# Transposing float32 q and k of the first head pair on TensorE without casts, in an attention and ELU feed-forward kernel

## The chip, the cores and the metric

The kernel runs on one core of a Trainium2 chip. A core has TensorE (PE; matmuls, and transposes as matmuls against an identity, results into PSUM), VectorE (DVE), ScalarE (ACT), GpSimd (POOL), SyncE (SP), and 16 DMA engines that all queues share. The metric is the device time of one execution in microseconds. Before the change it is 305.96 us, the median of three runs (305.51 to 306.67).

## The reference

The inputs are float32: q, k and v of shape (8, 8, 576, 64), that is batch, heads, sequence and head dimension, and two weights, w_in (512, 2048) and w_out (2048, 512).

```
scores = scale * q @ k^T                      # per batch and head
local heads 0-3:   0 <= i - j < 32
strided heads 4-7: i >= j and i % 32 == j % 32
attn = softmax(where(mask, scores, -1e9)) ;  a = attn @ v
x = a.transpose(0, 2, 1, 3).reshape(4608, 512)
h = x @ w_in ;  g = where(h > 0, h, exp(min(h, 0)) - 1)
out = g @ w_out                               # (4608, 512) float32
```

## The kernel before, in words

The program is written out by hand. The text `ORDER` is a list of tokens; the loop at its end calls one small function for each token, and each engine executes its instructions in the order in which the tokens issue them. Nothing is scheduled after that: an engine waits where an input or a buffer isn't ready, and everything behind on the same engine waits with it.

A key such as `0s1` names a pair of heads: batch 0, strided (`s`) or local (`l`), pair 1 of two. For the first two batches q and k are transposed on TensorE (`T`, function `transposes`) and copied out of PSUM to `qT` and `kT` as bfloat16 by VectorE (`c`) or ScalarE (`C`). `S` makes scores (L453), `e` the exponential on ScalarE (L460), `m` the mask on VectorE, `O` the products with ones and v, `n` and `r` a logarithm and an exponential that give the reciprocal of the sums (L551, L556), and `x` multiplies it in and writes `xT` in bfloat16 (L581). Layer 1 (`a` with rows 2 and 3 of `xT`, then `b` with rows 0 and 1, or both in `L`; L608) and layer 2 (`Z`, L642) go over 9 chunks of 512 tokens. The later attention pairs are mixed in between them. `D` tokens issue loads on POOL's queue, which also turn float32 into bfloat16 on the way.

The very first pair, `0s0`, does not wait for POOL's queue. Its q and k are loaded as float32 in two halves each, q by SP's queue and k by ACT's, into `stage`, memory of the later `g[0]` (L293 to L297). Four casts (`K` and `k`, function `cast`, L388) turn the halves into bfloat16 in `qs` and `ks`: q's first half and both halves of k on ScalarE, q's second on VectorE. The second half of k is cast ahead of the first. A half is transposed by four matmuls of 72 columns with the data as the weights (L401) and copied by L421. The other strided pair, `0s1`, is loaded as bfloat16 by POOL's queue ahead of everything else there.

`w` tokens (function `warm`, L385) are matmuls of zeros into a bank that is free. They compute nothing. A number is its columns, so `w.0.512.200` is two of them into bank 0. Eight of 512 columns open the program, and more stand between the steps up to the first `a`.

PSUM has 8 banks of 2 KiB for each partition, and the last number of a `T`, `S` or `O` token names the bank or banks. Four bfloat16 transposes of a half fill 288 columns of 2 bytes.

Of the kernel before, what the change touches and what calls it, by code (L numbers as in the profile page):

```python
# [8 lines left out]
F32 = mybir.dt.float32  # L9
BF16 = mybir.dt.bfloat16  # L10
I32 = mybir.dt.int32
ALU = mybir.AluOpType
# [23 lines left out]
w.7.512.512.512.512.512.512.512.512 D.ql.0.1 F.vp D.kl.0.1 F.v1 D.ql.0.0 k.q.0 F.ms D.vs.0.0 T.0s0.q.0.7  # L36
D.kl.0.0 K.q.1 K.k.1 D.vs.0.1 K.k.0 C.0s0.q.0 w.0.512.512.512.512.512 T.0s0.k.0.6 D.vl.0 T.0s0.k.1.5
T.0s0.q.1.4 c.0s0.k.0 T.0s1.k.7 c.0s0.k.1 c.0s1.k w.0.324 T.0s1.q.6 c.0s0.q.1 D.wi1.0 S.0s0.0.01 c.0s1.q
S.0s0.1.23 e.0s0.0 w.5.185 S.0s1.0.45 D.qs.1 S.0s1.1.67 e.0s1.0 m.0s0.0 w.2.224.224 T.0l1.k.1 D.wi3.0
e.0s1.1 m.0s1.0 w.0.499 T.0l0.q.0 C.0l1.k D.wi0.0 m.0s1.1 T.0l1.q.7 e.0s0.1 c.0l1.q w.4.155 O.0s0.0.16  # L40
D.wi2.0 c.0l0.q n.0s0.0 w.4.314 S.0l1.1.45 S.0l1.0.23 m.0s0.1 F.mk r.0s0.0 T.0l0.k.7 O.0s0.1.60 e.0l1.1
x.0s0.0 D.wo0.0 F.ml e.0l1.0 w.0.224.224.102 O.0s1.1.15 c.0l0.k n.0s0.1 D.wo1.0 w.4.247 O.0s1.0.43
n.0s1.1 m.0l1.0 n.0s1.0 r.0s1.1 D.ql.1 w.2.512.512.108 S.0l0.0.23 x.0s1.1 e.0l0.0 V.0 w.7.512.331
S.0l0.1.01 r.0s1.0 m.0l1.1 r.0s0.1 w.7.512 O.0l1.0.75 m.0l0.0 e.0l0.1 O.0l1.1.32 x.0s1.0 n.0l1.0 m.0l0.1
w.2.224.224 O.0l0.0.10 n.0l1.1 x.0s0.1 r.0l1.0 w.1.142 O.0l0.1.54 r.0l1.1 x.0l1.0 D.ks.1 n.0l0.0
w.4.224.224 a.0.5.6 x.0l1.1 n.0l0.1 a.0.7.7 r.0l0.0 a.0.4.0 r.0l0.1 x.0l0.0 a.0.6.4 D.kl.1 x.0l0.1
T.1s1.q.3 b.0.5 c.1s1.q b.0.7 h.0.5 b.0.4 h.0.7 i.0.5 b.0.6 h.0.4 g.0.5 T.1s0.q.5 D.wo2.0 a.0.12.3
C.1s0.q i.0.4 a.0.13.6 h.0.6 g.0.4 a.0.14.5 b.0.12 a.0.15.2 h.0.12 b.0.15 j.0.6 D.vs.1 a.0.2.1 j.0.12
b.0.13 g.0.6 b.0.2 h.0.13 g.0.12 a.0.1.4 h.0.2 i.0.7 b.0.1 i.0.13 a.0.3.3 g.0.7 h.0.1 D.wo3.0 b.0.3
i.0.2 b.0.14 h.0.3 g.0.2 a.0.0.7 j.0.1 b.0.0 a.0.11.1 g.0.1 h.0.0 a.0.10.0 h.0.14 D.vl.1 i.0.0 b.0.10  # L50
j.0.3 g.0.0 b.0.11 h.0.10 a.0.8.4 g.0.3 b.0.8 h.0.11 g.0.13 Z.0.0.0.7 h.0.15 i.0.10 D.ks.2 i.0.14
Z.0.0.1.7 h.0.8 g.0.10 j.0.11 Z.0.3.0.6 j.0.15 g.0.11 D.vs.2 Z.0.3.1.6 g.0.15 g.0.14 a.0.9.3 D.qs.2
i.0.8 b.0.9 g.0.8 Z.0.1.0.5 h.0.9 j.0.9 T.1s0.k.4 D.kl.2 Z.0.1.1.5 C.1s0.k g.0.9 T.1s1.k.2 S.1s0.1.01
c.1s1.k T.1l1.k.4 e.1s0.1 T.1l1.q.3 c.1l1.k T.1l0.q.2 S.1s1.0.01 m.1s0.1 Z.0.3.2.6 e.1s1.0 C.1l1.q
m.1s1.0 Z.0.1.2.5 C.1l0.q O.1s1.0.43 T.1l0.k.2 n.1s1.0 S.1s1.1.01 c.1l0.k Z.0.0.2.7 e.1s1.1 r.1s1.0
S.1s0.0.01 S.1l1.1.23 x.1s1.0 e.1s0.0 Z.0.1.3.5 m.1s1.1 m.1s0.0 e.1l1.1 Z.0.0.3.7 q.0.1 m.1l1.1 D.kl.3
S.1l0.1.01 S.1l1.0.23 V.1 e.1l0.1 Z.0.3.3.6 q.0.0 e.1l1.0 O.1l1.1.54 X.ks.2 m.1l1.0 O.1s0.1.73 n.1l1.1
m.1l0.1 S.1l0.0.01 n.1s0.1 Z.0.2.0.2 q.0.3 r.1l1.1 r.1s0.1 x.1l1.1 e.1l0.0 O.1s0.0.64 x.1s0.1 O.1l1.0.53
W.2 n.1s0.0 O.1l0.1.71 n.1l1.0 Z.0.2.1.2 m.1l0.0 r.1s0.0 X.qs.2 n.1l0.1 x.1s0.0 r.1l1.0 D.ql.2
O.1s1.1.04 r.1l0.1 x.1l1.0 O.1l0.0.63 n.1s1.1 x.1l0.1 Z.0.2.2.2 n.1l0.0 r.1s1.1 r.1l0.0 Z.0.2.3.2  # L60
x.1s1.1 X.kl.2 x.1l0.0 L.1.12.7 t.0.1 L.1.6.6 h.1.12 i.1.12 L.1.3.5 h.1.6 D.ks.3 i.1.6 L.1.4.4 h.1.3
D.vl.2 g.1.6 L.1.1.3 g.1.12 h.1.4 i.1.3 L.1.5.6 h.1.1 g.1.3 D.vs.3 L.1.13.7 i.1.4 h.1.5 i.1.1 i.1.5
L.1.0.5 h.1.13 g.1.5 D.qs.3 o.0.2 L.1.7.1 g.1.1 j.1.13 D.ql.3 g.1.4 h.1.0 L.1.2.6 X.ql.2 h.1.7 g.1.13
L.1.10.0 j.1.0 i.1.7 h.1.2 g.1.7 L.1.14.7 t.0.2 h.1.10 g.1.0 j.1.2 S.2s1.0.12 S.2s1.1.34 i.1.10 t.0.0
L.1.8.5 g.1.2 e.2s1.1 e.2s1.0 g.1.10 L.1.15.6 t.0.3 h.1.8 m.2s1.1 m.2s1.0 h.1.14 S.2s0.0.01 S.2s0.1.23
X.ks.3 L.1.9.4 e.2s0.1 i.1.14 g.1.14 h.1.15 L.1.11.3 e.2s0.0 i.1.15 h.1.9 Z.1.3.0.7 g.1.15 h.1.11 i.1.8
Z.1.3.1.7 j.1.9 g.1.8 m.2s0.1 O.2s1.1.01 Z.1.2.0.2 i.1.11 n.2s1.1 g.1.9 O.2s0.1.56 r.2s1.1 g.1.11
Z.1.2.1.2 n.2s0.1 x.2s1.1 Z.1.3.2.7 r.2s0.1 m.2s0.0 O.2s1.0.01 x.2s0.1 Z.1.2.2.2 n.2s1.0 O.2s0.0.34
r.2s1.0 Z.1.3.3.7 n.2s0.0 x.2s1.0 Z.1.2.3.2 r.2s0.0 q.1.3 S.2l0.0.01 S.2l0.1.56 x.2s0.0 Z.1.1.0.7
e.2l0.0 q.1.2 e.2l0.1 m.2l0.0 S.2l1.0.01 S.2l1.1.34 X.qs.3 Z.1.1.1.7 m.2l0.1 e.2l1.0 e.2l1.1 m.2l1.0  # L70
O.2l0.0.56 O.2l0.1.01 X.kl.3 n.2l0.0 m.2l1.1 Z.1.0.0.4 n.2l0.1 Z.1.0.1.4 r.2l0.0 t.1.3 O.2l1.1.23
r.2l0.1 x.2l0.0 Z.1.0.2.4 n.2l1.1 x.2l0.1 O.2l1.0.56 r.2l1.1 Z.1.0.3.4 X.ql.3 n.2l1.0 x.2l1.1 Z.1.1.2.7
r.2l1.0 D.qs.4 Z.1.1.3.7 x.2l1.0 D.kl.4 q.1.0 L.2.11.6 W.3 S.3s0.0.01 S.3s0.1.23 h.2.11 L.2.3.5 e.3s0.1
i.2.11 g.2.11 L.2.7.4 D.ks.4 h.2.3 o.1.1 D.vl.3 i.2.3 L.2.2.6 m.3s0.1 e.3s0.0 g.2.3 L.2.5.7 h.2.7 h.2.2
i.2.7 L.2.4.5 h.2.5 g.2.7 j.2.2 i.2.5 L.2.9.3 m.3s0.0 h.2.4 D.vs.4 g.2.5 L.2.0.4 h.2.9 g.2.2 j.2.4
D.ql.4 L.2.14.7 i.2.9 h.2.0 g.2.4 O.3s0.1.01 h.2.14 g.2.9 L.2.10.6 n.3s0.1 i.2.0 L.2.6.5 i.2.14 h.2.10
g.2.0 r.3s0.1 L.2.8.3 i.2.10 X.ks.4 g.2.14 h.2.6 L.2.13.4 x.3s0.1 h.2.8 j.2.6 g.2.10 O.3s0.0.01 X.qs.4
L.2.1.7 n.3s0.0 i.2.8 g.2.6 L.2.15.6 r.3s0.0 g.2.8 t.1.0 h.2.1 L.2.12.5 x.3s0.0 h.2.15 X.kl.4 i.2.1
S.3s1.0.01 S.3s1.1.23 g.2.1 e.3s1.1 Z.2.1.0.7 e.3s1.0 m.3s1.1 i.2.15 h.2.13 m.3s1.0 S.3l0.0.01
S.3l0.1.23 h.2.12 g.2.15 Z.2.1.1.7 e.3l0.1 i.2.12 j.2.13 Z.2.1.2.7 g.2.12 e.3l0.0 g.2.13 O.3s1.1.23  # L80
S.3l1.0.01 S.3l1.1.56 m.3l0.1 n.3s1.1 Z.2.1.3.7 m.3l0.0 e.3l1.1 Z.2.0.0.4 e.3l1.0 m.3l1.1 r.3s1.1
m.3l1.0 O.3s1.0.01 q.2.1 O.3l1.1.56 Z.2.0.1.4 n.3l1.1 x.3s1.1 t.2.1 n.3s1.0 Z.2.3.0.7 r.3l1.1 X.ql.4
O.3l1.0.23 Z.2.0.2.4 r.3s1.0 x.3l1.1 n.3l1.0 x.3s1.0 Z.2.3.1.7 t.1.2 r.3l1.0 S.4s1.0.01 S.4s1.1.56
x.3l1.0 t.1.1 Z.2.0.3.4 e.4s1.1 e.4s1.0 m.4s1.1 O.3l0.1.23 O.3l0.0.56 q.2.0 n.3l0.1 Z.2.3.2.7 W.4
r.3l0.1 Z.2.2.0.4 m.4s1.0 D.vs.5 n.3l0.0 x.3l0.1 O.4s1.1.01 D.ks.5 r.3l0.0 Z.2.2.1.4 D.vl.4 n.4s1.1
x.3l0.0 Z.2.3.3.7 r.4s1.1 L.3.14.6 x.4s1.1 D.qs.5 L.3.2.5 h.3.14 q.2.3 D.vl.5 i.3.14 S.4l0.0.01
S.4l0.1.23 h.3.2 L.3.7.7 g.3.14 e.4l0.0 i.3.2 e.4l0.1 L.3.11.6 D.kl.5 g.3.2 h.3.7 m.4l0.0 S.4s0.0.01
S.4s0.1.23 h.3.11 m.4l0.1 L.3.1.5 e.4s0.1 X.ks.5 e.4s0.0 Z.2.2.2.4 m.4s0.1 i.3.7 j.3.11 m.4s0.0
O.4s0.1.01 Z.2.2.3.4 g.3.11 n.4s0.1 g.3.7 O.4s0.0.23 r.4s0.1 L.3.0.6 n.4s0.0 x.4s0.1 D.ql.5 L.3.5.7
r.4s0.0 q.2.2 h.3.1 L.3.4.1 x.4s0.0 h.3.5 X.qs.5 L.3.6.4 j.3.1 i.3.5 h.3.0 g.3.5 L.3.15.0 h.3.6 g.3.1  # L90
t.2.0 h.3.4 L.3.12.7 i.3.0 h.3.15 g.3.0 t.2.2 L.3.3.5 j.3.4 i.3.6 h.3.12 g.3.4 L.3.8.6 h.3.3 g.3.6 j.3.3
O.4l0.1.12 i.3.12 L.3.10.3 n.4l0.1 g.3.3 L.3.9.4 i.3.15 h.3.8 g.3.15 h.3.10 L.3.13.5 g.3.12 r.4l0.1
h.3.9 Z.3.0.0.0 x.4l0.1 j.3.9 i.3.10 Z.3.2.0.7 D.qs.6 h.3.13 g.3.10 j.3.8 D.ks.6 Z.3.0.1.0 g.3.9 g.3.8
O.4l0.0.12 Z.3.2.1.7 i.3.13 n.4l0.0 X.kl.5 g.3.13 Z.3.0.2.0 r.4l0.0 x.4l0.0 S.5s0.0.34 S.5s0.1.56
Z.3.0.3.0 e.5s0.1 m.5s0.1 S.4l1.0.12 S.4l1.1.56 o.3.0 Z.3.2.2.7 e.4l1.1 e.4l1.0 Z.3.1.0.0 m.4l1.1 X.ql.5
# [638 lines left out]
```

## Time and profile before

| what | value |
|---|---|
| median of the runs, and their spread | 305.96 us, 305.51 to 306.67 |
| the profiled execution | 306.22 us, its span 304.5 us |
| TensorE busy | 297.1 us, 98% of the span |
| VectorE, ScalarE busy | 226.2 us (74%), 228.5 us (75%) |
| first dense layer-1 matmul starts | 18.62 us |
| zero matmuls | 35, from 1.3 to 18.5 us |

The span runs from the core's first to its last instruction; the execution's time is 1.72 us longer. In the lines of a timeline, the first number is the start in microseconds from the beginning of the span, the second the time that the instructions took, then come engine, line of the kernel, operation, and output and input with shape and type; "x2" is a group of two. A bracket gives the idle time of the engine ahead of it and what ended it. In the chain that ended last, a row is start, length, and the engine and line, or the transfer, that the chain passes through. A matmul's time includes its way through the array, so that those in a row overlap.

### The profile page before, as it was taken

How to read it: one execution, taken by the hardware profiler on the slowest of the kernel's cores; microseconds unless marked ns; L12 is line 12 of the kernel's file. 1: busy time of each engine (PE TensorE's matmuls, PEld its weight loads, DVE VectorE, ACT ScalarE, POOL GpSimd, SP SyncE). 2: the span in 40 equal slices, each digit the busy share in tenths (PEclk: the TensorE clock that was granted, in tenths of full speed). 3: DMA queues.
4: the chain of work that ended last, by engine and by line, in shares of the span. 5: the costliest groups of instructions: out<-in, count | busy, mean ns of one | idle time of the engine just before them, and what ended most of it. 6: DMA issues, size and time to landing. Idle time of an engine off the chain costs nothing.

```text
span 304.5 us, 6258 instructions
## 1 busy us (share of the span) xinstructions
PE 297.1 (98%) x2339; PEld 146.8 (48%) x2339; DVE 226.2 (74%) x435; ACT 228.5 (75%) x412; POOL 80.2 (26%) x110
## 2 busy tenths in 40 slices
PE   6999999999999999999999999999999999999994
PEld 2654455445544454445544554445444544444444
DVE  6777968798779978896788878976788358895020
ACT  4778678598879888997989889978777559982101
POOL 8922436830471008530188250000000000000000
PEclk9999999999999999999999999999999999999999
DMA  8999999999899759999899499801120022000053
GB/s 165 190 206 207 207 193 169 169 198 204 158 158 168 128 123 134 162 192 171 196 154 154 61 132 149 195 16 56 38 69 0 2 69 69 2 1 0 4 155 119
DMA packets 107358, 37.63 MB, mean 124 GB/s; under 512 B 89152, under 2 KB 102848, under 8 KB 107328
## 3 DMA queue, kind: packets, MB, share of 16 engines
q0 software_dynamic: 69728, 19.47, 62.3%
q1 hardware_dynamic: 36920, 17.08, 28.4%
q10 hardware_dynamic: 680, 0.69, 0.8%
q8 instruction: 18, 0.29, 0.4%
q14 instruction: 12, 0.10, 0.1%
HBM read 39.53 MB, written 9.44 MB: 161 GB/s over the span
## 4 chain that ended last, share of the span: by engine, by line
PE 86%; DVE 6%; ACT 3%; issue 2%; DMA 2%; ACTq 0%; DVEq 0%
PE ps L642 40%; PE ps L608 33%; PE ps L453 4%; DVE g L636 3%; DVE he L625 2%; PE ps L523 2%; PE ps L516 2%; DMA g<-in_k_dram 2%; PE ps L385 1%; PE ps L672 1%; ACT he L616 1%; PE ps L411 1%; PE ps L496 1%; PE ps L480 1%; ACT ln L551 0%
## 5 line engine op out<-in xcount | busy, mean ns | idle before, releaser
L642 PE MATMUL ps<-w_out_sb,g 128*128 128x512 bf16 x560 | 132.8, 379 | 0.5 <-DVE g L636 0.5
L608 PE MATMUL ps<-xT,w_in_sb 128*128 128x512 bf16 x576 | 130.5, 379 | 0.2 <-DVE g L634 0.2
L616 ACT ACTIVATE he<-ps 128x512 f32<-128x512 f32 x144 | 80.9, 596 | 22.2 <-PE ps L608 20.0
L608 PEld LDWEIGHTS <-w_in_sb 128*128 128x128 bf16 x576 | 55.0, 98 | 64.3 <-issue 1.1
L642 PEld LDWEIGHTS <-g 128*128 128x128 bf16 x560 | 51.1, 98 | 55.7 <-issue 0.8
L636 DVE TENSOR_TENSOR g<-he,ps 128x512 bf16<-128x512 bf16 x92 | 62.0, 684 | 1.9
L581 DVE TENSOR_TENSOR xT<-ps,ln 64x576 bf16<-64x576 f32 (+1 forms) x64 | 42.6, 678 | 20.3 <-ACT ln L556 19.4
L460 ACT ACTIVATE e<-ps 72x576 bf16<-72x576 f32 (+1 forms) x64 | 39.1, 647 | 12.7 <-PE ps L453 11.9
L625 DVE TENSOR_SCALAR he<-he 128x512 bf16<-128x512 f32 x92 | 40.2, 446 | 7.5 <-ACT he L616 6.8
L551 ACT ACTIVATE ln<-ps 64x576 f32<-64x576 f32 (+1 forms) x64 | 36.3, 583 | 10.0 <-PE ps L523 5.0
L634 DVE SCALAR_TENSOR_TENSOR g<-he,ps 128x512 bf16<-128x512 bf16 x52 | 34.8, 682 | 7.2 <-ACT he L623 6.9
L556 ACT ACTIVATE ln<-ln 64x576 f32<-64x576 f32 (+1 forms) x64 | 38.5, 619 | 1.2
L623 ACT ACTIVATE he<-he 128x512 bf16<-128x512 f32 x52 | 32.5, 630 | 1.3 <-DVE g L636 0.8
L648 DVE COPY osb<-ps 128x512 f32<-128x512 f32 x22 | 15.1, 685 | 16.3 <-PE ps L642 16.0
L243 POOL DMA_DIRECT2D ql<-in_q_dram x24 | 20.1, 840 | 7.7 <-DMA vl<-in_v_dram 4.1
L648 ACT COPY osb<-ps 128x512 f32<-128x512 f32 x13 | 7.6, 586 | 17.9 <-PE ps L642 14.1
L250 POOL DMA_DIRECT2D kl<-in_k_dram x24 | 17.8, 747 | 11.4 <-DMA w_out_sb<-in_moe_w_out_dram 3.7
L473 DVE TENSOR_TENSOR pm<-e,mask_l 128x576 bf16<-128x576 bf16 x32 | 14.1, 453 | 6.9 <-ACT e L460 5.3
L467 DVE TENSOR_TENSOR pm<-e,mask_s 72x576 bf16<-72x576 bf16 x32 | 14.2, 451 | 4.3 <-ACT e L460 4.1
L260 POOL DMA_DIRECT2D vl<-in_v_dram x8 | 9.8, 1220 | 9.5 <-PE ps L523 7.2
L233 POOL DMA_DIRECT2D vs<-in_v_dram x8 | 5.2, 652 | 25.6 <-DVE vsp L588 24.7
L516 PEld LDWEIGHTS <-vsp 72*128 72x128 bf16 x192 | 9.1, 98 | 5.5 <-issue 0.4
(93 smaller groups left out, 153.2 us busy)
## 6 DMA issues: line engine op xcount, KB each, us to landing
out_dram<-osb SPq DMA_DIRECT2D x30, 144.0 KB
vl<-in_v_dram POOLq DMA_DIRECT2D x8, 288.0 KB, 8.9
w_in_sb<-in_moe_w_in_dram POOLq DMA_DIRECT2D x4, 512.0 KB, 13.1
w_out_sb<-in_moe_w_out_dram POOLq DMA_DIRECT2D x4, 512.0 KB, 16.8
kl<-in_k_dram POOLq DMA_DIRECT2D x24, 72.0 KB, 7.3
ql<-in_q_dram POOLq DMA_DIRECT2D x24, 72.0 KB, 8.4
ks<-in_k_dram POOLq DMA_DIRECT2D x5, 320.0 KB, 8.2
vs<-in_v_dram POOLq DMA_DIRECT2D x5, 320.0 KB, 9.1
```

Of the source, the lines that this page charges most:

```text
L460: nc.scalar.activation(e[0:R], tiles.pop(("S", key, u))[0:R], ACT.Exp, scale=scale)
L551: nc.scalar.activation(t, s_ps, ACT.Ln)
L556: nc.scalar.activation(t, t, ACT.Exp, scale=-1.0)
L581: nc.vector.tensor_mul(dst, o_ps, rc)
L608: nc.tensor.matmul(tiles["h", ch, m], lhsT=w_in_sb[:, c, m * 128:(m + 1) * 128], rhs=xT[:, c, ch * CHUNK:(ch + 1) * CHUNK], start=(c == 2) ...
L616: nc.scalar.activation(e, tiles["h", i[0], i[1]], ACT.Exp)
L623: nc.scalar.activation(e1, e, ACT.Relu, bias=1.0, scale=-1.0)
L625: eng.tensor_scalar(e1, e, scalar1=1.0, scalar2=1.0, op0=ALU.min, op1=ALU.subtract)
L634: nc.vector.scalar_tensor_tensor(dst, e1, -1.0, h, op0=ALU.mult, op1=ALU.max)
L636: nc.vector.tensor_tensor(dst, e1, h, op=ALU.max)
L642: nc.tensor.matmul(ops, lhsT=g[ch % 2][:, m, kk * 128:(kk + 1) * 128], rhs=w_out_sb[:, m, :], start=(m == 0), stop=(m == MC - 1), skip_gro ...
L648: eng(o_sb, tiles.pop(("o", int(ch), int(kk))))
```

## The change

q and k of pair `0s0` are no longer cast. `transposes` takes the float32 halves straight from `stage`, with a float32 identity of 72 x 72 (a memset on VectorE and a select on POOL, issued at the start), and writes float32 into PSUM: 288 columns of 4 bytes, a bank for each half. The copies out of PSUM stay and now also turn float32 into bfloat16. There are still four transposes to a half. In `ORDER`:

- the four cast tokens go;
- `T.0s0.k.0` moves up behind `T.0s0.q.0`, ahead of the second halves, and its copy `c.0s0.k.0` with it;
- banks of the opening's transposes change (for example `T.0s0.k.1` from 5 to 7, `T.0s1.k` from 7 to 5);
- the zero matmuls are set anew: 1196 columns between the two halves (2560 before), 712 ahead of `T.0s1.k` (0), 774 ahead of `T.0s1.q` (324), 351 between the scores of `0s0` and `0s1` (185), and from there to the first `a` 5001 columns in place of 5738. Two of 224 columns behind `O.0l0.1` go altogether, and others lose some columns or their last piece.

The scores of pair `0s0` use 72 columns of `kT` as weights instead of 128, so that a block doesn't reach into the next half. A few tokens further back move by a place in the text, which leaves the order on every engine as it was. `load` gets a case for halves of w_in that no token uses.

```diff
 ORDER = """
-w.7.512.512.512.512.512.512.512.512 D.ql.0.1 F.vp D.kl.0.1 F.v1 D.ql.0.0 k.q.0 F.ms D.vs.0.0 T.0s0.q.0.7
-D.kl.0.0 K.q.1 K.k.1 D.vs.0.1 K.k.0 C.0s0.q.0 w.0.512.512.512.512.512 T.0s0.k.0.6 D.vl.0 T.0s0.k.1.5
-T.0s0.q.1.4 c.0s0.k.0 T.0s1.k.7 c.0s0.k.1 c.0s1.k w.0.324 T.0s1.q.6 c.0s0.q.1 D.wi1.0 S.0s0.0.01 c.0s1.q
-S.0s0.1.23 e.0s0.0 w.5.185 S.0s1.0.45 D.qs.1 S.0s1.1.67 e.0s1.0 m.0s0.0 w.2.224.224 T.0l1.k.1 D.wi3.0
+w.7.512.512.512.512.512.512.512.512 D.ql.0.1 F.vp D.kl.0.1 F.v1 D.ql.0.0 F.ms D.vs.0.0 T.0s0.q.0.7
+D.kl.0.0 T.0s0.k.0.6 C.0s0.q.0 D.vs.0.1 c.0s0.k.0 w.0.512.512.172 T.0s0.k.1.7 T.0s0.q.1.6 c.0s0.k.1
+D.vl.0 w.0.512.200 T.0s1.k.5 c.0s1.k c.0s0.q.1 w.0.512.262 T.0s1.q.7 D.wi1.0 S.0s0.0.01 c.0s1.q
+S.0s0.1.23 e.0s0.0 w.4.351 S.0s1.0.45 D.qs.1 S.0s1.1.67 e.0s1.0 m.0s0.0 w.2.224.224 T.0l1.k.1 D.wi3.0
...
+    identity_f = consts.tile([RS, RS], F32, tag="identity_f", name="identity_f")
...
+    nc.vector.memset(identity_f, 1.0)
...
+    nc.gpsimd.affine_select(
+        identity_f, identity_f, compare_op=ALU.is_equal, fill=0.0,
+        base=0, pattern=[[1, RS]], channel_multiplier=-1)
...
-    def cast(eng, nm, i):
-        n, f = "qk".index(nm), 2 * NS * D
-        eng(half(raw[nm + "s"][0:RS, 0:f], int(i)), half(stage[0:RS, n * f:(n + 1) * f], int(i)))
-
     def transposes(key, nm, *a):
         P, bank, part = Pair(key), int(a[-1]), a[:-1]
-        t = ps[:, bank, :].bitcast(BF16)[:, 0:S // (1 + len(part))]
+        t = ps[:, bank, 0:W] if part else ps[:, bank, :].bitcast(BF16)[:, 0:S]
...
         if part:
+            n = "qk".index(nm) * 2 * NS * D
+            src = stage[0:RS, n:n + 2 * NS * D].rearrange("p (h f) -> p h f", h=2)
             for i in range(NS // 2):
...
-                nc.tensor.transpose(t[:, i * RS:(i + 1) * RS], src[:, P.head(x), c0:c0 + 2 * D],
-                                    identity[0:RS, 0:RS])
+                nc.tensor.transpose(t[:, i * RS:(i + 1) * RS], src[:, x, c0:c0 + 2 * D], identity_f)
...
-                nc.tensor.matmul(dst, lhsT=P.kT[pr, k0:k0 + 128], rhs=rhs, start=True, stop=True,
+                n = RS if key == "0s0" else 128
+                nc.tensor.matmul(dst[0:n], lhsT=P.kT[pr, k0:k0 + n], rhs=rhs, start=True, stop=True,
                                  skip_group_check=True)
```

## The prediction, made before the changed kernel was run

> **What bounds the kernel now.** I read the page's busy shares first, then the chain that ended last, first whole and then cut to the first 34 us, then the timelines of each engine up to layer 1, and last POOL's waits, which tell when loads landed.
>
> ```profile
> span 304.5 us, 6258 instructions
> PE 297.1 (98%) x2339; PEld 146.8 (48%) x2339; DVE 226.2 (74%) x435; ACT 228.5 (75%) x412; POOL 80.2 (26%) x110
> PE 86%; DVE 6%; ACT 3%; issue 2%; DMA 2%; ACTq 0%; DVEq 0%
> ...
> 1.29 4.75 DMA g<-in_k_dram
> 6.07 1.15 ACT ks L390 x2
> 7.26 0.32 PE ps L401 x4
> 7.60 0.52 DVE kTs L421 x2
> 8.19 0.36 DVE kTs L427
> ...
> 8.57 0.31 DVE qTs L421
> 8.92 0.31 PE ps L453 x8
> ```
>
> TensorE is 98% busy and carries 86% of the chain: what the opening loses, the end loses. The opening is another thing. Up to 8.92 us the chain is a transfer of k (lands at 6.04), two casts on ScalarE, four transposes, and four copies on VectorE; TensorE only fills in. From 8.92 us on the chain is TensorE without a break, but zero matmuls (L385) stand in it, and those only pass time.
>
> ```profile
> 5.61 0.42 DVE L390 CAST qs<-g 72x512 bf16<-72x512 f32 x1
> 8.78 0.45 DVE L425 COPY qTs<-ps 128x576 bf16<-128x576 bf16 x1
> 9.69 1.18 ACT L460 ACTIVATE e<-ps 72x576 bf16<-72x576 f32 x2 [0.28 <-PE ps L453]
> 15.36 0.65 ACT L460 ACTIVATE e<-ps 128x576 bf16<-128x576 f32 x1 [0.21 <-PE ps L453]
> 19.27 0.76 ACT L556 ACTIVATE ln<-ln 128x288 f32<-128x288 f32 x2
> 19.74 0.95 DVE L581 TENSOR_TENSOR xT<-ps,ln 128x288 bf16<-128x288 f32 x2 [0.50 <-ACT ln L556]
> 17.86 0.64 POOL L233 DMA_DIRECT2D xT<-in_k_dram  x1 [2.95 <-DMA w_in_sb<-in_moe_w_in_dram]
> 22.39 0.75 POOL L278 DMA_DIRECT2D w_out_sb<-in_moe_w_out_dram  x1 [2.29 <-DMA w_in_sb<-in_moe_w_in_dram]
> ```
>
> Behind those zeros the real bound from 9.69 to 20 us is ScalarE: in 12.13 to 18.53 us it is busy for 6.03 of 6.40 us (VectorE 5.57), and its next exponential follows the last at once but for waits of 0.28 and 0.21 us. Its last reciprocal (19.27 + 0.76) frees the last xT product, which ends at 19.74 + 0.95 = 20.69; the second half of the first layer-1 tile (`b.0.5`) needs it and starts at 20.77, though the transposes before it were issued by 20.61. So the start of dense layer 1 is set by ScalarE and VectorE, by 0.1 to 0.2 us. POOL's waits date the weights: wi1 by 17.86 us (first use 18.53), wi3 by 22.39 (first use 22.90).
>
> **The change part by part.** *Casts.* Three on ScalarE (0.62 and 1.15 us) and one on VectorE (0.42) go. On the path is the 1.15 us, 6.07 to 7.21. The other 0.62 and the 0.42 lie beside the wait for k and pay nothing.
>
> *Sixteen float32 transposes* take the place of sixteen bfloat16 ones. Each is still one matmul with one weight load of 128 columns. The trace has no float32 matmul, so the price p is bounded: below by the bfloat16 ones, issued every 33 ns (a group of four in 0.13 us); above by four passes of a weight load that nothing overlaps, 4 x 98 ns (mean of the LDWEIGHTS rows) = 0.39 us. I take 0.10 us, the row that it is nearest to: one pass, with a weight load that is not sped up. The Trainium skill, page "TensorE: Matmul & The Clock Gate", section on weight-path perf modes, says that the fast weight load is not used for FP32, and its LDWEIGHTS section gives columns / 1.2, from which an estimate of 107 ns follows; no trace here shows it yet, and by it the sum below would stay within 0.05 us.
>
> *New timeline up to the scores.* The eight opening zeros end at 4.76 (1.26 + 3.50, unchanged). q's first half is there at 4.28. k's first half was issued first on its queue and the trace's landing record has it at 4.62. So `T.0s0.q.0` and `T.0s0.k.0` run 4.76 to 5.56 (8 x 0.10). Zeros of 512 + 512 + 172 columns at 0.42 ns (512 columns every 0.215 us) take 0.50: 6.06. k's second half lands at 6.04, so `T.0s0.k.1` and `T.0s0.q.1` run 6.09 to 6.89. Zeros of 712 columns: 0.30, 7.19. Now `T.0s1.k` meets another load: ks of heads 6 and 7 is issued at 2.13 and takes 5.1 us, 7.2. It starts at 7.25; before, it started at 7.62. This is the new wait, and all of TensorE stands behind it.
>
> From its first weight load to its copy took 0.57 us before (7.62 to 8.19): the copy starts at 7.82 and the next (`c.0s0.q.1`) 0.38 later, 8.20. That one now reads float32 from PSUM. Bounds: 0.22 us until the next copy starts, as before (8.57 to 8.79), or 288/512 of the 0.685 us of the float32 output copies, 0.39; I take 0.33. So `c.0s1.q` starts at 8.53 and ends at 8.98 instead of 9.23. `T.0s1.q`, behind zeros of 774 columns, has ended by 8.3 and doesn't bind. Gain at `S.0s1.0`, hence at ScalarE's exponential at 9.69: 0.25 us, with the quick copy 0.36. I carry 0.3.
>
> *Narrower scores of the first pair* (72 weight columns, not 128): 16 weight loads. The 64-column loads of L411 are issued every 24 ns, the 128-column ones every 33, so nothing to 0.1 us of gain on TensorE, which waits there for VectorE: 0. The dependence on the second half, which the 128 columns had, goes too; but `S.0s0.0` still stands behind `T.0s1.q` in TensorE's order.
>
> *Fewer zeros behind the scores.* 166 columns more before `S.0s1`, 737 fewer from there to `a.0.5`: 0.31 us of TensorE. Bounds 0 and 0.31. I take 0, because ScalarE is back to back and its work isn't less; only the wait of 0.21 us at 15.36, for scores behind zeros that shrink by 108 columns (0.05 us), can give a little.
>
> *A new identity.* VectorE sets 72x72 float32 (some 0.1 us, next to the 0.17 of the 128x128), POOL fills it (0.20 to 0.31, from the iota and the first identity), in front of six attention loads, vl, and the weights. Of POOL's queue, qs and ks are issued ahead of it. The rest start 0.2 to 0.3 later, but they land 5.0 us after issue, then 9 to 16: they queue behind each other, and from 3.0 us the DMA share is at 1 or above. Cost 0; uncovered it would be 0.25 us at wi1, whose slack is 0.67. Every other DMA and every other instruction keeps its place on its queue, SP's included.
>
> *Loads that an earlier TensorE could meet.* kl lands at 3.87 + 5.0 to 5.6 (used at 10.00), vs at 5.08 + 5.6 (11.52), wi1 at 17.86 (18.53), wi3 at 22.39 (22.90). The least slack is about 0.5 us: 0.3 passes, and no more than 0.5 can.
>
> Sum: ScalarE's chain, `b.0.5` and all that follows start 0.3 us sooner; later stages are the same instructions in the same order. The profiled run took 306.22 (span 304.5 plus 1.72), 0.26 over the median of 305.96: 305.9 for that run, 305.65 against the median.
>
> **The rivals.** *Float32 transposes too dear (slower).* Place: between 6.09 and `T.0s1.k`. All 16 stand in TensorE's order ahead of it, so it starts at 4.76 + 0.80 + 16p if that is later than 7.25. Up to p = 0.105 nothing changes, at about 0.125 the gain is gone, and every further 10 ns cost 0.16. At the upper bound of 0.39: 305.96 + 16 x 0.265 = 310.2. For it: four bytes for two. Against: one weight load and one matmul each. The Trainium skill speaks both ways: "FP8 and Floating Point Precision", in its TensorE notes, gives true FP32 four passes, while the terms of "TensorE: Matmul & The Clock Gate" call the transpose mode four times faster for FP32; the first would put p near the upper bound, the second near what I take. No run here shows either yet.
>
> *The zeros count in full.* Then 0.3 + 0.31, cut by wi3 to 0.5: 305.45. Against it the ScalarE rows above.
>
> *No gain arrives* because ks lands 0.3 later or the copies of float32 are slower: 305.96.
>
> *The clock falls back.* The opening zeros took 0.43 us each, later ones 0.215: TensorE starts at half speed. Between 4.76 and 8.4 zeros fall from 2884 to 2682 columns. Should the gate not see enough work, 3.5 us at half speed cost up to 1.7 us: 307.4. Page "TensorE: Matmul & The Clock Gate", Part 4, says that transposes don't count as busy; by zeros alone 1.21 us against 1.13 hardly differ, so it has little chance.
>
> **How the numbers follow.** Forecast 305.65: 0.63. Zeros in full 0.09. No gain 0.10. Dear transposes 0.13, half of them beyond 1.5 us. Clock 0.05. What a measurement of this kernel tells from no change is about 0.5%, 1.5 us. No named case is that much faster; 0.04 for what I don't see. Slower by that: half of the dear transposes and some of the clock, 0.09. Same: 0.87. Range: the runs of before spread over 305.5 to 306.7; 305.0 takes in the zeros in full with half that spread, 306.7 the cheaper half of the dear transposes.
>
> **What would show it.** No casts at L390; eight float32 transposes over some 0.8 us from 6.1; `T.0s1.k` at 7.2 to 7.3, released by the load of ks; the exponential of L460 now at 9.69 at about 9.4; `b.0.5` at about 20.45, still behind xT of VectorE; the same stages after that, 0.3 earlier. Wrong if the transposes are issued further apart than 0.12 us, if zeros run at 0.43 us after 5 us, or if a w_in wait shows on TensorE before 23 us.

## The result, and the profile after

The changed kernel takes 306.59 us in the median of 20 runs (305.99 to 308.29), the kernel before 305.93 in 20 runs beside it. The ratio, worked out from all these runs and not from the two medians, is 1.0028, with a 95% interval of 1.0018 to 1.0038. That is some 0.85 us slower, where 0.3 us faster was forecast. The time lies within the range that I gave, but by luck: its upper end, 306.7, stands for dear transposes, which did not come. The sign is wrong.

The two profiled executions hide this: 306.22 us before and 306.21 after, with the same span. The one of before is 0.29 us above the median of its runs, the one of after 0.38 below. What follows is therefore read from the places where the traces differ, and every verdict on time from many runs.

From the page of the changed kernel: span, busy engines, the busiest DMA queue (packets, MB, and the time that its packets took as a share of 16 engines' span), and the chain by engine.

```profile
span 304.5 us, 6251 instructions
PE 297.1 (98%) x2336; PEld 147.1 (48%) x2336; DVE 225.5 (74%) x435; ACT 226.8 (74%) x409; POOL 81.0 (27%) x111
q0 software_dynamic: 69728, 19.47, 72.0%
PE 82%; DMA 13%; DVE 2%; POOL 1%; issue 1%; ACTq 0%; DVEq 0%
```

The busy shares are as before. Two lines are not. Transfers carry 13% of the chain, against 2% before; but in the second profile of the changed kernel (`after_again` below, an execution of 306.89 us) they carry 2% again, so this share belongs to one execution. And queue q0, which holds POOL's loads, took 72.0% with 69728 packets and 19.47 MB; before it was the same packets and bytes in 62.3%. This one repeats: 71.4% and 63.1% in the second profiles. Nothing more is moved, but moving it takes longer.

The same chain of the changed kernel, cut to the first 48 us (start, length, what):

```profile
1.28 4.70 DMA g<-in_k_dram
6.12 0.46 PE ps L405 x4
6.67 0.47 DVE kTs L424
7.23 1.19 POOL vl L261
...
11.28 16.39 DMA w_in_sb<-in_moe_w_in_dram
...
27.95 17.07 DMA w_out_sb<-in_moe_w_out_dram
...
45.07 1.89 PE ps L646 x8
```

The casts are gone from the opening, as they should be. From 7.23 us on the chain is no longer TensorE but POOL's queue of loads: the issue of vl, then w_in, then w_out, whose last block lands at 45.03 and lets TensorE go on at 45.07.

TensorE, ScalarE, VectorE and POOL of the changed kernel, from their timelines (start, length, engine, line, operation; in brackets the idle time ahead of it and what ended it):

```profile
6.12 0.70 PE L405 MATMUL ps<-identity_f,g 72*128 72x72 f32 x8 [0.49 <-DMA g<-in_k_dram]
6.65 0.47 PE L391 MATMUL ps<-zero 128*128 128x512 bf16 x2
7.29 0.43 PE L411 MATMUL ps<-identity,ks 72*128 72x72 bf16 x8 [0.17 <-DMA ks<-in_k_dram]
16.70 0.31 PE L500 MATMUL ps<-pm,ones 128*64 128x288 bf16 x1 [0.41 <-issue]
20.81 1.02 PE L612 MATMUL ps<-xT,w_in_sb 128*128 128x512 bf16 x4
45.07 1.24 PE L646 MATMUL ps<-w_out_sb,g 128*128 128x512 bf16 x5 [0.46 <-DMA w_out_sb<-in_moe_w_out_dram]
```

```profile
9.50 1.18 ACT L464 ACTIVATE e<-ps 72x576 bf16<-72x576 f32 x2 [0.24 <-PE ps L457]
16.82 0.65 ACT L464 ACTIVATE e<-ps 128x576 bf16<-128x576 f32 x1 [0.45 <-DVE pm L477]
```

```profile
15.69 0.55 DVE L589 COPY vl<-vl 32x1472 bf16<-32x1472 bf16 x1 [0.30 <-DMA vl<-in_v_dram]
19.82 0.94 DVE L585 TENSOR_TENSOR xT<-ps,ln 128x288 bf16<-128x288 f32 x2 [0.50 <-ACT ln L560]
```

```profile
15.95 0.65 POOL L234 DMA_DIRECT2D xT<-in_q_dram  x1 [1.49 <-DMA vl<-in_v_dram]
18.73 0.64 POOL L234 DMA_DIRECT2D xT<-in_k_dram  x1 [2.14 <-DMA w_in_sb<-in_moe_w_in_dram]
22.92 0.94 POOL L280 DMA_DIRECT2D w_out_sb<-in_moe_w_out_dram  x1 [1.93 <-DMA w_in_sb<-in_moe_w_in_dram]
```

The opening did gain: the second exponential starts at 9.50 (9.69 before). At 15.69 it is gone. There VectorE copies the rows of v of the local heads that two blocks share (`V.0`, within the tiles `vl`), and it waits 0.30 us for vl's load; before, it started at 15.67 and waited for nothing. The masks stand behind it in VectorE's order. ScalarE's next exponential waits 0.45 for one of them, and `b.0.5` starts at 20.81 (20.75 before). TensorE has a gap of 0.41 in the middle of a pair of products; its row names no releaser ("issue"), and the section on addresses comes back to it. POOL's issues, which wait for earlier loads to land, stand at 18.73 and 22.92 where they stood at 17.86 and 22.39.

### The profile page after: what moved, and what is told of

Read it like the earlier page. It is cut to its first block, busy times and chain, and to the rows that moved or that the text cites. A ratio compares the mean times of both kernels' runs of the same rounds, so it can differ in the third digit from the quotient of the medians.

```text
span 304.5 us, 6251 instructions
## 1 busy us (share of the span) xinstructions
PE 297.1 (98%) x2336; PEld 147.1 (48%) x2336; DVE 225.5 (74%) x435; ACT 226.8 (74%) x409; POOL 81.0 (27%) x111
## 3 DMA queue, kind: packets, MB, share of 16 engines
q0 software_dynamic: 69728, 19.47, 72.0%
## 4 chain that ended last, share of the span: by engine, by line
PE 82%; DMA 13%; DVE 2%; POOL 1%; issue 1%; ACTq 0%; DVEq 0%
PE ps L646 38%; PE ps L612 35%; DMA w_out_sb<-in_moe_w_out_dram 6%; DMA w_in_sb<-in_moe_w_in_dram 5%; PE ps L457 3%; PE ps L527 2%; PE ps L520 2%; DMA g<-in_k_dram 2%; PE ps L676 1%; DVE g L640 1%; POOL w_in_sb L276 1%; POOL vl L261 0%; DVE he L629 0%; DVE xT L585 0%; POOL xT L234 0%
## 5 line engine op out<-in xcount | busy, mean ns | idle before, releaser
L464 ACT ACTIVATE e<-ps 72x576 bf16<-72x576 f32 (+1 forms) x64 | 39.1, 647 | 15.6 <-PE ps L457 14.5
L629 DVE TENSOR_SCALAR he<-he 128x512 bf16<-128x512 f32 x92 | 39.2, 435 | 7.8 <-ACT he L620 7.4
L251 POOL DMA_DIRECT2D kl<-in_k_dram x24 | 17.9, 751 | 15.2 <-DMA w_out_sb<-in_moe_w_out_dram 4.5
L652 ACT COPY osb<-ps 128x512 f32<-128x512 f32 x13 | 7.6, 586 | 17.9 <-PE ps L646 14.1
L477 DVE TENSOR_TENSOR pm<-e,mask_l 128x576 bf16<-128x576 bf16 x32 | 14.1, 454 | 7.0 <-ACT e L464 5.4
```

The source lines that it names most:

```text
L464: nc.scalar.activation(e[0:R], tiles.pop(("S", key, u))[0:R], ACT.Exp, scale=scale)
L629: eng.tensor_scalar(e1, e, scalar1=1.0, scalar2=1.0, op0=ALU.min, op1=ALU.subtract)
L652: eng(o_sb, tiles.pop(("o", int(ch), int(kk))))
```

## The experiments

All times are ratios to the kernel before, run beside each kernel on its chip (its medians were 305.70 to 305.93 us), with a 95% interval.

### The same kernels again, and the two parts that were in doubt

`after_again` and `before_again` are the two kernels unchanged.

> The changed kernel unaltered, for a second profile of it. Theory A (loads): the opening is 0.2 to 0.3 us earlier again, but vl of batch 0 lands at 15 us or later (13.97 before) and a w_out load ends a wait of TensorE at about 45 us, because the float32 identity's select puts all loads behind it later on POOL. Time 306.2 to 307. Theory B (chance): the late landings differ from run to run; in this profile vl lands near 14 and no transfer stands in the chain after 10 us, while the time is still 306.2 to 307. Theory C (zeros): the loss sits in TensorE between 9 and 18.5 us whatever lands when.

> The kernel before unaltered, for a second profile. Theory A: vl lands at about 14, wi1 at about 17.6, the last of the 16 engines within 2.2 us of the first for each load, no wait for w_out. Theory B: landings spread as in the changed kernel, by 0.7 us or more, in a run of 305.9.

`e1_identity_dve` takes the float32 identity off POOL; VectorE copies it from the bfloat16 one later in the opening.

```diff
-    nc.vector.memset(identity_f, 1.0)
...
-    nc.gpsimd.affine_select(
-        identity_f, identity_f, compare_op=ALU.is_equal, fill=0.0,
-        base=0, pattern=[[1, RS]], channel_multiplier=-1)
...
+            nc.vector.tensor_copy(identity_f, identity[0:RS, 0:RS])
```

> The changed kernel, but VectorE copies the float32 identity from the bfloat16 one after vs_p's ones are set, so POOL has no select for it and issues its loads as before. Theory A: loads land as before (vl near 14, wi1 near 17.6), the gain of 0.2 to 0.3 us in the opening stays, 305.6 to 305.8. Theories B and C: no different from the changed kernel, 306.2 to 307.

`e2_zeros_only` is the kernel before with the changed kernel's zero matmuls from behind the scores of `0s1` to the first `a`.

```diff
-e.0s1.1 m.0s1.0 w.0.499 T.0l0.q.0 C.0l1.k D.wi0.0 m.0s1.1 T.0l1.q.7 e.0s0.1 c.0l1.q w.4.155 O.0s0.0.16
+e.0s1.1 m.0s1.0 w.0.483 T.0l0.q.0 C.0l1.k D.wi0.0 m.0s1.1 T.0l1.q.7 e.0s0.1 c.0l1.q w.4.147 O.0s0.0.16
...
```

> The kernel before with its casts, but with the smaller zero matmuls from the third step of batch 0's attention to layer 1 as the changed kernel has them (737 columns fewer; the zeros up to the scores of 0s1 stay). Theory A: no change, 305.9, since ScalarE sets that stretch. Theory C: slower by most of the 0.7 us, 306.4 or more.

Measured: after_again 1.0027 (1.0014 to 1.0040), before_again 0.9996 (0.9987 to 1.0005), e1 1.0021 (1.0008 to 1.0035), e2 1.0004 (0.9994 to 1.0015). The loss repeats on another chip, so it is no accident of a few runs. It stays without the select on POOL: theory A falls. The fewer zeros make no difference that can be measured, by themselves: theory C falls, and the prediction's 0 for them stands.

What the changed kernel and e1 share, and e2 does not have, is not an instruction. `identity_f` is a tile of 72 float32, 288 bytes in each partition, and it stands ahead of `ones`, `qs`, `ks`, `ql`, `kl`, `vs`, `vl`, `vsp` and the rest, so all these tiles moved by 288 bytes. Before, each of these that a load fills begins on a multiple of 128 bytes; now it begins 32 bytes beyond a multiple of 64. In the opening, `vl` is the load with the smallest pieces, 2304 of 128 bytes. That became theory D.

### Addresses alone

`e3_identity_in_g1` (and `e3_again`) is the changed kernel with the float32 identity in memory that is idle at that time, so that no tile moves.

```diff
-    identity_f = consts.tile([RS, RS], F32, tag="identity_f", name="identity_f")
+    identity_f = g[1][0:RS, MC - 1, 0:2 * RS].bitcast(F32)
```

> The changed kernel, with the float32 identity put into the last row of g[1], memory that is not used before layer 1 of the second chunk, in place of a tile of its own. Every other tile then lies at the address that it has in the kernel before; the opening, the zeros and the select on POOL stay as changed. Theory D (the new tile of 288 bytes moves all later tiles by 288, from multiples of 64 bytes to 32 beyond one, and POOL's loads into them land later): vl lands as before, at about 14.0 us, w_in's second block at about 17.5, and the opening's 0.3 us is seen at the end: 305.6 us, ratio 0.999. Theory B (the landings differ from one program to the next for other reasons): 306.6 us as the changed kernel, vl at 15.2 to 15.8. Theory E (the earlier opening brings the loads into a collision, whatever the addresses): 306.6 us, vl late.

> The changed kernel with the float32 identity in g[1] once more, to narrow its interval. Theory D with F: 305.8 us, ratio 1.000, the moved tiles' cost gone and the opening's gain given back. If the opening's gain is kept in part: 305.6 us, ratio 0.999.

`e4_shift_288` and `e5_shift_320` are the kernel before with an unused tile (144 or 160 columns of bfloat16), and no other edit.

```diff
     identity = consts.tile([128, 128], BF16, tag="identity", name="identity")
+    pad = consts.tile([128, 144], BF16, tag="pad", name="pad")
```

> The kernel before with one unused tile of 288 bytes behind the bfloat16 identity. Nothing else differs, no instruction is added. Theory D: vl lands at 15.2 to 15.8 us and the time rises by 0.7 to 1.1 us (the loss of the changed kernel and the 0.3 us of its opening that the loss had eaten): 306.6 to 307.0 us, ratio 1.003. Theories B and E: 305.9 us, ratio 1.000.

> The kernel before with one unused tile of 320 bytes behind the bfloat16 identity: later tiles move, and stay on multiples of 64 bytes (though no longer of 128). Theory D with 64 bytes as the step that matters: 305.9 us, ratio 1.000, vl at about 14.0 us. If 128 bytes is the step, or any move of the tiles costs: 306.6 us or more, vl late. Theories B and E: 305.9 us.

`e6_shift_vl` (32 bytes) and `e8_shift_vl_128` (128 bytes) move only the vl tiles of the kernel before; `e7_vl_back` puts only the vl tiles of the changed kernel back on a multiple of 128. The edit shown is that of e6; e7 and e8 have unused tiles of other sizes in the same places.

```diff
+    pad0 = consts.tile([128, 16], BF16, tag="pad0", name="pad0")
     vl_t = [consts.tile([128, (2 * HG * LB + 1) * D], BF16, tag=f"vl{i}", name=f"vl{i}")
             for i in range(2)]
+    pad1 = consts.tile([128, 16], BF16, tag="pad1", name="pad1")
```

> The kernel before with an unused tile of 32 bytes ahead of the two vl tiles and another behind them: the vl tiles alone lie 32 bytes beyond a multiple of 64, all others stay on multiples of 64. Theory D, with the 2304 elements of 128 bytes of vl as the load that suffers: vl lands late, 15.2 us or more, and the time is 306.6 us, ratio 1.002 or more. Theory D with all loads sharing the cost: between, 306.1 to 306.4. Theories B and E: 305.9 us.

> The changed kernel with an unused tile of 96 bytes ahead of the two vl tiles and one of 32 behind them: the vl tiles alone are back on multiples of 128 bytes, all other tiles stay 32 bytes beyond a multiple of 64. Theory D with vl as the load that suffers: vl lands at 14.0 to 14.6 us and the time comes back to 305.7 to 305.9, ratio 1.000. Theory D with every moved load sharing the cost: 306.2 to 306.5, ratio 1.002.

> The kernel before with 128 unused bytes ahead of the two vl tiles and 128 behind: they move, and their 128-byte pieces stay on multiples of 128. If the step that matters is 128 bytes: vl at about 14.0 us, 305.8 us, ratio 1.000. If the step is 256 bytes, or if any move of vl costs: vl at 15.2 or later, 306.3 us, ratio 1.002.

Measured, with the share of q0 from each page and the GB/s that the core's DMA engines moved from 13.0 to 14.5 us, right behind vl's pieces:

| kernel | vl tiles begin | others begin | ratio (95%) | q0 | GB/s |
|---|---|---|---|---|---|
| before | on 128 | on 128 | 1 | 62.3% | 207 |
| e2 | on 128 | on 128 | 1.0004 (0.9994–1.0015) | 61.8% | 202 |
| changed, identity in g[1]: e3 | on 128 | on 128 | 1.0002 (0.9993–1.0010) | 64.5% | 197 |
| the same again: e3_again | on 128 | on 128 | 1.0003 (0.9994–1.0012) | 63.2% | 194 |
| before, vl +128: e8 | on 128 | on 128 | 1.0006 (0.9997–1.0015) | 62.1% | 203 |
| changed, vl back: e7 | on 128 | 32 off | 1.0011 (1.0000–1.0023) | 64.9% | 199 |
| before, vl +32: e6 | 32 off | on 128 | 1.0022 (1.0011–1.0033) | 66.7% | 173 |
| before, all +288: e4 | 32 off | 32 off | 1.0028 (1.0017–1.0040) | 67.8% | 168 |
| before, all +320: e5 | 64 off | 64 off | 1.0024 (1.0014–1.0033) | 70.5% | 171 |
| e1 | 32 off | 32 off | 1.0021 (1.0008–1.0035) | 71.0% | 163 |
| changed | 32 off | 32 off | 1.0028 (1.0018–1.0038) | 72.0% | 177 |

The stretch from 13.0 to 14.5 us in the kernel before, in e6 and in e8 (busy times by engine, then the clock, the DMA share and GB/s):

```profile
13.00:14.50 1.50, 1.50 (x35) 1.10 (x32) 1.50 (x6) 1.50 (x5) 1.50 (x3) 1.00 1.43 207
```

```profile
13.00:14.50 1.50, 1.50 (x33) 1.06 (x26) 1.50 (x6) 1.50 (x5) 1.22 (x2) 1.00 1.69 173
```

```profile
13.00:14.50 1.50, 1.50 (x33) 1.06 (x26) 1.50 (x6) 1.50 (x5) 1.18 (x2) 1.00 1.47 203
```

Theory D is shown, and theories B and E, by which addresses don't matter, fall with e4. An unused tile of 288 bytes costs as much as the whole change (e4, 1.0028); taking the identity's tile away gives the loss back (e3, 1.0002); moving vl alone by 32 bytes gives 1.0022, and putting vl alone back leaves 1.0011, whose interval begins at 1. So vl carries most of it, and what the other moved tiles add lies within the intervals. A multiple of 64 is not enough (e5), one of 128 is (e8). In the two rows of e6 and e8, the DMA engines are busier and move less while the target is off the boundary: a DMA share of 1.69 for 173 GB/s in e6, 1.47 for 203 in e8. Over all twenty profiles the GB/s part the two groups, 194 to 207 on the boundary against 159 to 177 off it; the DMA share does not.

The trace's packet records say a little more. vl's own packets take 32 ns in the mean in all these kernels. The 1024-byte packets that follow them from 13.5 to 14.0 us take 98 ns in the kernels with vl on its boundary, and 151 to 191 ns in the mean in the others (up to 333), although they go to `w_in_sb`, which has not moved. I read this as vl's writes still being worked off then; that is argued, not shown.

One instruction fetch of 16 KB (queue q8) falls into the same time, and it parts the kernels as well: it took 0.97 to 0.98 us in the thirteen profiles with vl on its boundary, and 1.25 to 1.68 us in the seven with vl off it. TensorE may meet it. In after_again it stops between two matmuls of one pair:

```profile
16.24 0.31 PE L500 MATMUL ps<-pm,ones 128*64 128x288 bf16 x1
17.23 0.31 PE L500 MATMUL ps<-pm,ones 128*64 128x288 bf16 x1 [0.68 <-issue]
```

In before_again this pair starts at 16.27 and 16.29 us. In seven profiles its two starts lie 0.14 us or more apart, and six of the seven have vl off its boundary; there the second matmul starts 1.21 to 1.47 us after the fetch has landed. That the fetch brings TensorE's instructions, that TensorE waits for them, and that this is a second way in which the addresses cost time, is argued from the timing, not shown.

The Trainium skill has a rule that bears on this, on its page "DMA: Bandwidth & Descriptors", section "How a descriptor splits into AXI transactions": a transfer is cut into transactions that start on 256-byte boundaries, so a piece that lies across such a boundary takes one more. By it a 128-byte piece on a multiple of 128 never does. The section speaks of what a transaction reads; I apply it to the target, which is written. For batch 0, the pieces of vl begin 128 bytes beyond a multiple of 256 in the kernel before and on one in e8 and e7, and they lie across one in e4, e5 and e6. All agree with the rule, the changed kernel too, but no run here separates a boundary of 256 from one of 128. The section is about the cost of the transfer; it says nothing of the packets behind it.

One of my marks was poor. I had expected the landing of vl to part the kernels: 14.0 us against 15.2 or later. vl's last engine landed at 15.33, 15.37 and 15.14 in e7, e8 and e3_again too, a single engine, with the others done by 14.9. In these a 16 KB instruction fetch of 0.97 us started at 13.1 to 13.4 us, in the kernel before at 13.9; that it held this engine is argued, not shown. The first of the 16 engines parts the kernels: 12.9 to 13.2 us on the boundary, 13.5 to 14.1 off it.

### Why e3 does not gain

With no tile moved, e3 has `b.0.5` at 20.43, where I had put it (20.45), and still ends level with the kernel before. In its second profile, e3_again, `b.0.5` starts at 20.71 and the opening gains next to nothing (the point on the carried 0.3 us, below, says why). Theory F is about e3: near 30 us VectorE stands still while POOL issues its longest load. The instruction that stands is the clamp, which takes the ELU's exponential to min(e, 1) - 1. VectorE (two rows) and POOL (one) of e3:

```profile
30.20 0.95 DVE L629 TENSOR_SCALAR he<-he 128x512 bf16<-128x512 f32 x1
31.18 0.69 DVE L640 TENSOR_TENSOR g<-he,ps 128x512 bf16<-128x512 bf16 x1
```

```profile
29.73 1.19 POOL L261 DMA_DIRECT2D vl<-in_v_dram  x1 [1.94 <-DMA w_out_sb<-in_moe_w_out_dram]
```

Other clamps of this shape take 0.42 us. This one ends at 31.15, 0.23 us after the issue. In before_again TensorE is 0.3 us later, the clamp begins at 30.54, takes 0.58, and ends at 31.12. VectorE is level, and so is the layer-2 group that waits for it: 36.58 and 36.63. Three experiments take the collision away.

`e9_g1_vl1_later` (on e3) and `e10_before_vl1_later` (on the kernel before) exchange two of POOL's loads, so that a short issue comes first.

```diff
-... h.0.14 D.vl.1 i.0.0 ... h.0.15 i.0.10 D.ks.2 i.0.14 ...
+... h.0.14 D.ks.2 i.0.0 ... h.0.15 i.0.10 D.vl.1 i.0.14 ...
```

> The changed kernel with the float32 identity in g[1] (no tile moved), and the tokens of two of POOL's later loads exchanged: the long issue of v for batch 1 (1.19 us) takes the place of the short one of k for batch 2 (0.65 us) and the other way round. Theory F (the opening's 0.3 us is given back near 30 us, where VectorE's clamp stands still until POOL's 1.19 us issue is done): the clamp at 30.2 us takes about 0.4 us and not 0.95, the layer-2 group that started at 36.58 starts 0.2 to 0.3 earlier, and the time is 305.4 us, ratio 0.999. Rival G (it would be given back later anyway, at a wait that depends on the loads): the clamp is shorter, and the time stays at 305.8.

> The kernel before with the same two tokens exchanged, as the control. Theory F: VectorE is level with TensorE there, so that little comes of it: 305.7 us, ratio 0.999 to 1.000. Rival G: 305.8.

Measured: 1.0011 (1.0002 to 1.0020) and 1.0007 (0.9997 to 1.0018). VectorE and POOL of e9:

```profile
30.20 0.43 DVE L629 TENSOR_SCALAR he<-he 128x512 bf16<-128x512 f32 x1
...
32.46 1.45 DVE L629 TENSOR_SCALAR he<-he 128x512 bf16<-128x512 f32 x2
```

```profile
29.76 0.64 POOL L234 DMA_DIRECT2D ks<-in_k_dram  x1 [1.96 <-PE ps L612]
32.37 1.32 POOL L261 DMA_DIRECT2D vl<-in_v_dram  x1 [1.97 <-DVE g L638]
```

The clamp at 30.20 is short, as theory F has it. But the long issue then meets the next two clamps, which take 1.45 together (0.75 in e3): the first, which begins 0.09 us into the issue, takes its usual 0.42, the second 1.11. The group still starts at 36.60. The collision was moved, not removed.

`e11_g1_vl1_early` (on e3) and `e12_before_vl1_early` exchange `D.vl.1` with the earlier `D.vs.1`.

```diff
-... j.0.6 D.vs.1 a.0.2.1 ... h.0.14 D.vl.1 i.0.0 ...
+... j.0.6 D.vl.1 a.0.2.1 ... h.0.14 D.vs.1 i.0.0 ...
```

> The changed kernel with the float32 identity in g[1] (no tile moved), and POOL's load of the local v of batch 1 exchanged with that of its strided v: the 1.19 us issue then stands at 24.4 us, where VectorE is busy for only 2.6 of 5 us, and a 0.65 us issue at 29.7. Theory F (VectorE, standing still behind the long issue near 30 us, gives the opening's 0.3 us back): the clamps of 30 to 33 us take 0.4 to 0.55 and none 0.95, the layer-2 group of 36.58 starts at 36.2 to 36.4, and the time is 305.5 us, ratio 0.999. Rival G (given back later anyway, or at another wait): that group may start earlier, and the time is 305.9, ratio 1.000.

> The kernel before with the same two loads exchanged, as the control for the exchange itself. Theory F: TensorE is 0.3 us later there and VectorE waits for it, so little comes of it: 305.7 to 305.9 us, ratio 1.000. Rival G: 305.8.

`e13_after_wo3_early` does the like in the changed kernel, to see whether the wait for w_out at 45 us is the price.

```diff
-... j.0.6 D.vs.1 a.0.2.1 ... h.0.1 D.wo3.0 b.0.3 ...
+... j.0.6 D.wo3.0 a.0.2.1 ... h.0.1 D.vs.1 b.0.3 ...
```

> The changed kernel as it is (vl off its boundary), with w_out's last block exchanged with the load of strided v of batch 1 in POOL's queue, so that it lands about 1.6 us earlier (43.4 us in place of 45.0). Theory H (what the late queue costs is the wait for that block at 44.6 us, 0.46 us in the profile of the changed kernel): 306.1 us or less, ratio 1.001 or less. If the cost is met elsewhere (vl's own products at 16.3, w_out's third block, other loads): 306.5, ratio 1.0025.

All three missed: 1.0153 (1.0139 to 1.0166), 1.0151 (1.0128 to 1.0174) and 1.0063 (1.0050 to 1.0075). I had overlooked what else stands on the load that was put back. The strided v of batch 1 goes into `g` and is needed at 42.5 us. TensorE of e11, then of e13:

```profile
45.98 0.45 PE L493 MATMUL ps<-pm,g 72*64 72x72 bf16 x8 [3.51 <-DMA g<-in_v_dram]
```

```profile
43.77 0.32 PE L493 MATMUL ps<-pm,g 72*64 72x72 bf16 x8 [0.70 <-DMA g<-in_v_dram]
...
45.85 0.39 PE L646 MATMUL ps<-w_out_sb,g 128*128 128x512 bf16 x1
```

In e13 the wait for w_out is gone, and a wait of 0.70 us for v has taken its place. These runs tell nothing on theory F or H. They do show how little slack POOL's queue has: one place later costs 0.7 us, two places 3.5.

`e14_g1_g13_first` (on e3) and `e15_before_g13_first` move no load. They put an instruction of VectorE whose inputs are long ready into the time of the collision.

```diff
-... h.0.14 D.vl.1 i.0.0 b.0.10 j.0.3 g.0.0 b.0.11 h.0.10 a.0.8.4 g.0.3 b.0.8 h.0.11 g.0.13 Z.0.0.0.7 ...
+... h.0.14 D.vl.1 g.0.13 i.0.0 b.0.10 j.0.3 g.0.0 b.0.11 h.0.10 a.0.8.4 g.0.3 b.0.8 h.0.11 Z.0.0.0.7 ...
```

> The changed kernel with the float32 identity in g[1] (no tile moved), and one instruction of VectorE moved: the maximum of block 13 (inputs long ready) goes ahead of the clamp of block 0, into the time in which that clamp stands still behind POOL's 1.19 us issue of v. Theory F (with the table of all profiles: that clamp ends 0.22 to 0.23 us after the issue, and the layer-2 group at 36.6 follows 5.4 us later, whatever TensorE's lead): the clamp still ends at about 31.1, but one instruction of 0.6 us less follows it, so the group starts at 36.0 to 36.3 in place of 36.55 to 36.58, and the time is 305.4 to 305.6 us, ratio 0.998 to 0.999. Rival G (the lead is lost again at a later wait): the group starts earlier and the time is 305.9, ratio 1.000.

> The kernel before with the same instruction moved. Theory F: the group that started at 36.63 to 36.74 starts at 36.3 to 36.5, where TensorE itself is the limit, and the time is 305.6 to 305.7 us, ratio 0.999. Rival G: 305.8, ratio 1.000.

Measured: 1.0001 (0.9993 to 1.0010) and 1.0006 (0.9997 to 1.0015). VectorE of e14, and two groups of its TensorE:

```profile
30.13 0.68 DVE L640 TENSOR_TENSOR g<-he,ps 128x512 bf16<-128x512 bf16 x1
30.73 0.55 DVE L629 TENSOR_SCALAR he<-he 128x512 bf16<-128x512 f32 x1
```

```profile
36.38 1.03 PE L646 MATMUL ps<-w_out_sb,g 128*128 128x512 bf16 x4
...
97.77 0.42 PE L520 MATMUL ps<-pm,vsp 72*128 72x72 bf16 x8 [0.15 <-DVE xT L585]
```

The place behaves as theory F says: the clamp no longer stands in the way, and the group starts at 36.38. In this profile TensorE waits for VectorE again at 97.77, and that group starts where it does in before_again (97.79, an execution of 305.52 us); VectorE is without a break there from 95.1 us on. What makes VectorE late by 95 us in both kernels I did not look into.

By the times rival G holds. The spans on record, which every execution has beside its time, say something else. In all 22 executions of e14 and e15 the time is 2.05 to 2.15 us longer than the span; in those of every other kernel here it is 1.66 to 1.79. And the spans themselves are shorter than those of the kernel before on the same chip: 303.80 us in the mean against 304.15 in e14 (0.35 less, 95% interval 0.15 to 0.55), and 303.90 in e15 (0.25 less, 0.02 to 0.48). Those of e3 and e3_again are not (0.17 and 0.04 longer, within their intervals). So what this edit wins does reach the last instruction, by about as much as theory F had forecast, and some 0.37 us outside the span take it back; no trace here shows what these are. e15 wins nearly as much without the changed opening, so most of this is the worth of VectorE's new order; what e14 has beyond it, 0.1 us, lies within the noise.

## Why the prediction was wrong, point by point

**The failed step: "A new identity ... Cost 0; uncovered it would be 0.25 us at wi1 ... Every other DMA and every other instruction keeps its place on its queue".** I counted the identity's memset and select, and they do cost nothing that can be measured: e3 keeps both and lies at 1.0002. The order of the queues also stayed. But the tile itself shifts every tile behind it by 288 bytes, and no step of mine looked at addresses. The price, by e4, is 0.28%, 0.86 us, which is the whole result. It is none of the rivals: the slower ones that I named were dear transposes and the clock.

**The opening** went as worked out, in the profile of the changed kernel. `T.0s1.k` starts at 7.29 and is released by ks (forecast 7.25). The float32 transposes are cheaper than I took: eight of them from 6.12, the next group at 6.65, so 0.066 us each (taken 0.10, bounds 0.033 to 0.39). The four passes that the Trainium skill's "FP8 and Floating Point Precision" gives for true FP32, in its TensorE notes, do not show here. The next copy on VectorE starts 0.36 after `c.0s0.q.1` (taken 0.33).

**"I carry 0.3".** The exponential that started at 9.69 starts at 9.50 in this profile, 9.29 in e3, again at 9.69 in e3_again, and at 9.76 in after_again. The TensorE row of e3_again says why:

```profile
6.34 0.70 PE L405 MATMUL ps<-g,g 72*128 72x72 f32 x8 [0.40 <-DMA g<-in_k_dram]
```

The casts had stood between k's landing and TensorE; without them TensorE stands directly behind two loads, k (6.0 us in e3, 6.3 in this one) and ks (7.0 and 7.4), and the zero matmuls between them are on the path. The gain is between 0.4 us and nothing, by the execution. The rival "no gain arrives because ks lands 0.3 later" was this one, in part of the executions.

**Fewer zeros: 0.** Right: e2 at 1.0004. **Narrower scores: 0.** Nothing contradicts it; not tested by itself. **The clock** stayed at full speed in the page's rows behind the opening.

**"Loads that an earlier TensorE could meet. ... The least slack is about 0.5 us."** The slacks were read from landings of the kernel before and taken as fixed. They moved. In the profile of the changed kernel vl is met at 15.7 us (0.30 on VectorE) and w_out's last block at 44.6 (0.46 on TensorE). I had dated no landing of vl at all. No w_in wait showed before 23 us.

**"Later stages are the same instructions in the same order"**, so that a lead would last to the end. Also wrong, and it would have cost the forecast gain without the first error: the changed kernel without moved tiles lies at 1.0002 and 1.0003 (e3, e3_again), and at 1.0001 with the collision at 30 us taken out (e14, whose shorter span is told above). Where VectorE or a load sets the pace, TensorE's lead ends, though TensorE is 98% busy.

Where the slower executions of the changed kernel lose their time is known in part; e13 was to tell and did not. after_again's profile is of one of them (306.89 us). There `b.0.5` starts at 21.37, 0.6 us later than in before_again. VectorE's copy of vl waits for nothing; the row that stands out is TensorE's gap of 0.68 us between the two matmuls above. TensorE loses another half microsecond between 65 and 86 us, of which a wait of 0.22 us for an exponential at 80.5 us is one piece; w_out's last block is not met at all. The rest stays open.

By its time no kernel here beats the one before. e3 and e14 give the loss back and are level with it.

## What to carry to other kernels

A new tile is an edit to every tile allocated behind it: when a tile is added, compare the addresses that loads write to, and keep the targets of small pieces on a multiple of 128 bytes, or put the newcomer last or into memory that is idle. A first sign is the queue's line on the page: the same packets and bytes at a higher share of the engines' time. And a lead gained in the opening is only worth what no later engine and no load takes back; before summing it to the end, look for the first stage where another engine runs without a break. Compare the spans as well as the times: e14 and e15 are level by the one and shorter by the other.

## What the runs showed of the hardware that was not expected

- Loads into vl, in 128-byte pieces, to targets 32 or 64 bytes off a multiple of 128: the queue's share rises from 62.3% to 66.7% with vl alone moved, to 67.8–72.0% with all the tiles behind the new one, and the time by 0.21 to 0.28%. A 16 KB instruction fetch in the same stretch takes 1.25 to 1.68 us in place of 0.97.
- VectorE's float32-to-bfloat16 clamp stands still while POOL issues a load. In thirteen profiles the clamp near 30 us began 0.35 to 0.86 us into the 1.19 us issue of vl for batch 1, and it ended 0.22 to 0.23 us after the issue, whenever it had begun (0.55 to 1.06 us in place of 0.42); e3, e14 and before_again above are three of them. A clamp that began in the first 0.2 us of that issue was not held: in e6, e9 and e10 it took 0.42 to 0.43 us, and the issue took 1.32 to 1.42 us in place of 1.19. The elementwise maximum that took its place in e14 has its usual 0.68 beside such an issue (0.69 in e3). The Trainium skill, "SBUF — State Buffer", section "SBUF: two separate sides", describes one port pair that VectorE and GpSimd share as an exclusive lock, where the second waits until the first is done, and warns of VectorE holding up POOL's descriptors. The traces agree and show both directions: POOL's issue holds up VectorE for most of its length, and where a clamp began in its first 0.2 us the issue was the longer one.
- A float32 transpose of 72 columns on TensorE: 0.066 us each in a row of eight, against 0.033 for bfloat16 in the opening before.
